# Two of the last chunk's output stores issued by ScalarE in place of SyncE, in a fused S5 state-space and SwiGLU kernel

## The chip, the cores and the metric

The kernel runs on one core of a Trainium2 chip. The metric is the device time of one execution in microseconds; the median of several runs counts. Beside it stands one profiled execution, whose span runs from the program's first to its last instruction.

## What is computed

One sequence of 2048 tokens with 512 features, in bfloat16. The input x is layer-normalized, and the result is the sum of x, a state-space branch and a gated feed-forward branch. Cut to what matters:

```python
xn = layernorm(x)                                  # over the 512 features
# S5 branch: complex diagonal recurrence over time, 512 states
h[t] = Lam_bar * h[t-1] + B_bar @ xn[t]
ssm  = 2 * real(h @ C.T) + xn * Dskip
# feed-forward branch, 1376 hidden features
ffn  = (silu(xn @ w_gate) * (xn @ w_up)) @ w_down
out  = x + ssm + ffn
```

## The kernel before

The tokens are cut into four chunks of 512, and each chunk into four token tiles of 128 (`NT` is 16 tiles, `TPC` is 4 per chunk; tile `n` belongs to chunk `n // 4`). The normalized input is kept transposed in SBUF. For each chunk TensorE multiplies it with the gate and up weights (`gateup_tile`, line 446), and with the input matrix of the recurrence (`bproj_tile`, line 371). ScalarE moves those results out of PSUM and applies silu; VectorE multiplies gate and up, rotates the states, runs the scans over time (line 413) and rotates back. The order of all this is written out by hand: the kernel's last lines queue VectorE's work in pieces, and `pump` takes pieces from that queue beside TensorE's work.

The output of a token tile is a sum in one PSUM tile: the feed-forward products with `w_down` (lines 547, 559 and 587), and then in `out_ssm` (line 606) eight products with the output matrix of the recurrence. For the chunks 0 to 2, ScalarE copies the sum into an SBUF tile `res` (line 618) and GpSimd stores it with an accumulating DMA (line 619), onto x and the skip term that have been put there before.

The last chunk is done otherwise. `out_pair` (line 550) computes the feed-forward part of the chunks 2 and 3 first, then the state-space part of both. In the last chunk x and the skip term lie ready in SBUF (`xn_end`, and for half of the last tile `part_end`), and VectorE adds them as it takes the sum out of PSUM (line 611). The result in `res` is then stored by a plain DMA (line 613). Tiles 0 to 2 of this chunk (n = 12, 13 and 14) are 512 columns wide; the last, n = 15, is computed and stored in three pieces of 256, 128 and 128 columns (`out_blocks`, line 535), so that little is left to do behind its last product. The store of tile 0 is cut in two halves of 256 columns, which have the same piece to wait for.

Which engine issues a store of line 613 is set by its last column: a store that reaches the right edge of the tile (`b == D`) goes out through SyncE, another through ScalarE. Before the change, SyncE so issues the second half of tile 0, tile 1, tile 2 and the last piece of tile 3; ScalarE issues the first half of tile 0 and the first two pieces of tile 3:

```python
for a, b in ((0, D // 2), (D // 2, D)) if i == 0 else ((lo, hi),):
    (nc.sync if b == D else nc.scalar).dma_start(out=out_v[:, n, a:b], in_=res[:, a:b])
```

Each of these two engines has a DMA queue of its own (q1 and q10 in the profile). An engine issues its DMAs in the order of its program, and a DMA waits at its place for what it needs: here for VectorE's addition, and for the DMA that last used its completion semaphore. There are eight such semaphores ("lanes"), which the DMAs of SyncE and ScalarE take in turn, whichever of the two issues; the wait for the lane is an instruction of its own ahead of the DMA. At the program's end SyncE waits for all lanes one after the other, drains, and meets the other engines (these instructions stand under line 877, the launch).

Of the kernel before, what the change touches and what calls it, by code (L numbers as in the profile page):

```python
# [23 lines left out]
def kernel(  # L24
# [17 lines left out]
    nc = tc.nc  # L42
    _, L, D = A_x.shape
# [5 lines left out]
    NT = L // 128  # L49
    NCH = L // CW  # L50
    TPC = CW // 128
# [28 lines left out]
    out_v = out[0].rearrange("(n p) d -> p n d", p=128)  # L80
# [454 lines left out]
    def out_blocks(n):  # L535

        return ((0, D // 2), (D // 2, D - 128), (D - 128, D)) if n == NT - 1 else ((0, D),)
# [12 lines left out]
    def out_pair(c):  # L550

        multiply(0)
        for n in range(c * TPC, (c + 2) * TPC):
            o = bank()
            o_tiles[n] = [o]
            k, i = divmod(n, TPC)
            for lo, hi in col_parts(n):
                for fi in range(FT - 1):
                    nc.tensor.matmul(o[:, lo:hi], lhsT=gu_tiles[k][:, fi, i * 128:(i + 1) * 128],  # L559
                                     rhs=wd_sb[:, fi, lo:hi], start=(fi == 0), stop=False)  # L560
                if lo > 0:
                    out_last(n, o[:, lo:hi], lo, hi, True)
            pump(FT * 0.2163)
        for step in range(3):
            for k in (c, c + 1):
                out_rows(k, step)
        need(f"ssm{c}")
        need("skip")
        for n in range(c * TPC, (c + 1) * TPC):
            out_ssm(n)  # L570
            pump(2 * NQ * 0.2163)
        need(f"ssm{c + 1}")
        n = NT - 1
        o = o_tiles[n][0]
        V.tensor_tensor(out=part_end[:], in0=o[:, D // 2:D], in1=xn_end[:, TPC - 1, D // 2:D], op=ALU.add)
        o_tiles[n] = [o, *(bank((128, hi - lo)) for lo, hi in out_blocks(n)[1:])]
        for n in range((c + 1) * TPC, (c + 2) * TPC):
            out_ssm(n)
# [18 lines left out]
    def out_ssm(n):  # L597
        c, i = divmod(n, TPC)
        if c > 0:
            res = opool.tile([128, D], BF16, name="res")  # L600
        for o, (lo, hi) in zip(o_tiles[n], out_blocks(n)):
            fresh = n == NT - 1 and lo > 0
            o = o[:, 0:hi - lo]
            for part in range(2):
                for q in range(NQ):
                    nc.tensor.matmul(o, lhsT=w_tiles[c][:, part, q, i * 128:(i + 1) * 128],  # L606
                                     rhs=CF[:, part, q, lo:hi], start=(fresh and part == 0 and q == 0),
                                     stop=(c > 0 and part == 1 and q == NQ - 1))
            if c == NCH - 1:
                rest = part_end[:, lo - D // 2:hi - D // 2] if fresh else xn_end[:, i, lo:hi]  # L610
                V.tensor_tensor(out=res[:, lo:hi], in0=o, in1=rest, op=ALU.add)  # L611
                for a, b in ((0, D // 2), (D // 2, D)) if i == 0 else ((lo, hi),):
                    (nc.sync if b == D else nc.scalar).dma_start(out=out_v[:, n, a:b], in_=res[:, a:b])
            elif c > 0:
                out_leave(n, o, res)

    def out_leave(n, o, res):
        nc.scalar.copy(out=res[:], in_=o[:])  # L618
        nc.gpsimd.dma_start(out=out_v[:, n, :], in_=res[:], accum_op=ALU.add)  # L619
# [147 lines left out]
    def out_chunk(c):  # L767

        multiply(0)
        for n in range(c * TPC, (c + 1) * TPC):  # L770
            out_ffn(n)
            pump(FT * 0.2163)
        if c == 0:
            need("ln3")
            up_halves()
            multiply(0)
        need(f"ssm{c}")
        need("cf")
        for n in range(c * TPC, (c + 1) * TPC):
            out_ssm(n)  # L780
            pump(2 * NQ * 0.2163)
# [100 lines left out]
```

## Time and profile before

| | |
|---|---|
| Median of 3 runs | 179.2 us (179.16 to 179.3) |
| The profiled execution's own time | 179.75 us |
| Its span | 178.0 us |
| TensorE clock granted, mean | 0.998 |
| TensorE busy | 172.9 us, 97% |
| VectorE busy | 154.8 us, 87% |
| ScalarE busy | 93.8 us, 53% |
| GpSimd busy | 39.6 us, 22% |
| Line 613, DMA issues | 4 on SyncE, 3 on ScalarE |

The profile knows an engine by a short name: PE is TensorE's matmuls and PEld its weight loads, DVE is VectorE, ACT ScalarE, POOL GpSimd, SP SyncE. A name with a q behind it (ACTq, SPq) is the engine's sequencer: instructions that wait, branch or issue a DMA, which are not counted as busy time. Times inside the profile count from the start of the span. "PE ps L606" is a matmul of line 606 that writes a tile `ps`. The time to landing of a DMA runs from the start of its issue until all of its completion semaphore's increments are in.

### The profile page before, as it was taken

To read this page: it belongs to the slowest core of one execution; us is meant where nothing else is said; L and a number is where in the kernel's file an instruction comes from. 1 tells how busy PE (TensorE), PEld (TensorE's weight loads), DVE (VectorE), ACT (ScalarE), POOL (GpSimd) and SP (SyncE) were. 2 spreads that over 40 slices of the span, in tenths; PEclk is the share of its full clock that TensorE was granted. 3 is DMA by queue.
4 is the path that set the end of the run, shared out by engine and by line. 5 is a ranking of instruction groups with operands and counts; after the bars stand their busy time and mean duration, and the time that the engine had idled before them with its cause. 6 is when DMAs were issued, how large, how long until landed. Compare 5 with 4: busy or idle time off the path is not lost.

```text
span 178.0 us, 2494 instructions
## 1 busy us (share of the span) xinstructions
PE 172.9 (97%) x906; PEld 84.1 (47%) x922; DVE 154.8 (87%) x238; ACT 93.8 (53%) x167; POOL 39.6 (22%) x61
## 2 busy tenths in 40 slices
PE   8999999999999999999999999999999999999992
PEld 2984444444444444444444444444444444474452
DVE  6789997999999995999999999999999999990042
ACT  3468898867399559914966662013766600002300
POOL 6050300000300050000709340014276420002400
PEclk9999999999999999999999999999999999999999
DMA  5998656994041025900450020007479400000752
GB/s 169 305 266 224 131 89 158 349 212 103 17 88 33 0 35 112 353 0 0 54 68 15 9 64 28 0 0 63 55 113 183 79 7 0 0 0 4 80 99 61
DMA packets 30093, 16.13 MB, mean 91 GB/s; under 512 B 19296, under 2 KB 29888, under 8 KB 30048
## 3 DMA queue, kind: packets, MB, share of 16 engines
q1 hardware_dynamic: 25088, 11.80, 28.4%
q0 software_dynamic: 4416, 3.87, 15.6%
q10 hardware_dynamic: 576, 0.30, 0.5%
q8 instruction: 7, 0.11, 0.3%
q14 instruction: 6, 0.05, 0.1%
HBM read 8.42 MB, written 5.24 MB: 77 GB/s over the span
## 4 chain that ended last, share of the span: by engine, by line
PE 97%; issue 1%; DVE 0%
PE ps L446 36%; PE ps L606 15%; PE ps L371 15%; PE ps L559 10%; PE ps L587 10%; PE ps L694 3%; PE ps L671 2%; PE ps L501 2%; PE ps L490 1%; PE ps L594 1%; PE ps L547 1%; PE ps L236 1%; DVE res L611 0%; PE ps L266 0%
## 5 line engine op out<-in xcount | busy, mean ns | idle before, releaser
L446 PE MATMUL ps<-xnT,wg 128*128 128x512 bf16 x144 | 37.8, 379 | 0.4
L446 PE MATMUL ps<-xnT,wu 128*128 128x512 bf16 x145 | 37.3, 379 | 0.0
L413 DVE TENSOR_TENSOR_SCAN g<-r_t,car,u 128x512 bf16<-128x512 f32 x24 | 28.7, 1263 | 0.0
L371 PE MATMUL ps<-xnT,BT 128*128 128x512 bf16 x126 | 28.2, 379 | 0.1
L606 PE MATMUL ps<-CF,wt 128*128 128x512 bf16 (+2 forms) x140 | 27.8, 355 | 0.3 <-issue 0.2
L460 ACT ACTIVATE guT<-ps 128x512 bf16<-128x512 f32 x40 | 24.5, 612 | 6.7 <-PE ps L446 5.2
L461 ACT CAST u<-ps 128x512 bf16<-128x512 f32 x40 | 24.0, 599 | 5.4 <-PE ps L446 5.1
L618 ACT CAST res<-ps 128x512 bf16<-128x512 f32 x12 | 6.7, 594 | 37.5 <-PE ps L606 37.5
L619 POOL DMA_DIRECT2D out_dram<-res x12 | 10.5, 1043 | 59.2 <-ACT res L618 59.2
L446 PEld LDWEIGHTS <-wu 128*128 128x128 bf16 x148 | 14.5, 98 | 17.5
L446 PEld LDWEIGHTS <-wg 128*128 128x128 bf16 x148 | 14.4, 98 | 17.2
L373 ACT CAST u<-ps 128x512 bf16<-128x512 f32 x32 | 18.4, 589 | 5.1 <-PE ps L371 4.9
L606 PEld LDWEIGHTS <-wt 128*128 128x128 bf16 x144 | 13.4, 98 | 14.8 <-issue 0.4
L371 PEld LDWEIGHTS <-BT 128*128 128x128 bf16 x128 | 12.5, 98 | 15.1
L587 PE MATMUL ps<-wd_sb,guT 128*128 128x512 bf16 x78 | 18.0, 379 | 0.1
L559 PE MATMUL ps<-wd_sb,guT 128*128 128x512 bf16 (+1 forms) x89 | 17.5, 355 | 0.1
L211 POOL TENSOR_TENSOR rstd<-ve,neg_half 128x4 f32<-128x4 f32 x3 | 5.2, 1729 | 47.0 <-DVE ve L210 47.0
L186 POOL DMA_DIRECT2D gu_rows<-gu_last x24 | 11.9, 504 | 9.3 <-DVE gu_last L477 6.6
L465 DVE TENSOR_TENSOR guT<-guT,u 128x1024 bf16<-128x1024 bf16 x20 | 13.5, 681 | 0.0
L559 PEld LDWEIGHTS <-guT 128*128 128x128 bf16 x90 | 8.8, 98 | 8.7
L587 PEld LDWEIGHTS <-guT 128*128 128x128 bf16 x80 | 7.8, 98 | 9.4
L611 DVE TENSOR_TENSOR res<-ps,xn_end 128x512 bf16<-128x512 f32 (+1 forms) x4 | 2.5, 625 | 10.6 <-PE ps L606 10.6
(116 smaller groups left out, 199.0 us busy)
## 6 DMA issues: line engine op xcount, KB each, us to landing
out_dram<-in_A_x_dram SPq DMA_DIRECT2D x1, 1536.0 KB, 6.8
out_dram<-res POOLq DMA_DIRECT2D x12, 128.0 KB, 3.1
out_dram<-xall POOLq DMA_DIRECT2D x3, 512.0 KB, 8.2
wd_sb<-in_B_w_down_dram SPq DMA_DIRECT2D x1, 1280.0 KB, 9.8
xall<-in_A_x_dram SPq DMA_DIRECT2D x1, 1024.0 KB, 6.7
wg<-in_B_w_gate_dram SPq DMA_DIRECT2D x1, 512.0 KB, 5.0
wu<-in_B_w_up_dram SPq DMA_DIRECT2D x1, 512.0 KB, 6.0
xall<-in_A_x_dram SPq DMA_DIRECT2D x2, 256.0 KB, 6.1
```

The lines of the kernel that those rows point to most:

```text
L186: nc.gpsimd.dma_start(out=gu_rows[c % 2][i * RT:(i + 1) * RT, p, :], in_=gu_last[c % 3][p * RT:(p + 1) * RT, i * 128:(i + 1) * 128])
L371: nc.tensor.matmul(ps[:], lhsT=BT[:, part, k, q * 128:(q + 1) * 128], rhs=xnT[:, k, c * CW:(c + 1) * CW], start=(k == 0), stop=(k == KD - 1))
L373: nc.scalar.copy(out=u_tiles[c][:, part, q, :], in_=ps[:])
L413: V.tensor_tensor_scan(out=g()[:, part, q, :], data0=r_t[:, q:q + 1].to_broadcast([128, CW]), data1=u_tiles[c][:, part, q, :], initial=ini ...
L446: nc.tensor.matmul(ps[:fs, lo:hi], lhsT=wslice(groups, fi, k), rhs=xnT[:, k, c * CW + lo:c * CW + hi], start=(k == 0), stop=(k == KD - 1))
L460: nc.scalar.activation(out=guT[:fs, fi, :], in_=psg[:fs], func=ACT.Silu)
L461: nc.scalar.copy(out=u_pair[c][:fs, fi % 2, :], in_=psu[:fs])
L465: products.append(lambda: V.tensor_tensor(out=g, in0=g, in1=u, op=ALU.mult))
L559: nc.tensor.matmul(o[:, lo:hi], lhsT=gu_tiles[k][:, fi, i * 128:(i + 1) * 128], rhs=wd_sb[:, fi, lo:hi], start=(fi == 0), stop=False)
L587: nc.tensor.matmul(o[:], lhsT=gu_tiles[c][:, fi, i * 128:(i + 1) * 128], rhs=wd_sb[:, fi, lo:hi], start=(fi == 0), stop=False)
L606: nc.tensor.matmul(o, lhsT=w_tiles[c][:, part, q, i * 128:(i + 1) * 128], rhs=CF[:, part, q, lo:hi], start=(fresh and part == 0 and q == 0 ...
L619: nc.gpsimd.dma_start(out=out_v[:, n, :], in_=res[:], accum_op=ALU.add)
```

## The change

For line 613 the engine is chosen otherwise: SyncE keeps only the second half of tile 0 (n = 12) and the last piece of the last tile (n = 15); tile 1 and tile 2 (n = 13 and 14), each 128 rows of 1024 bytes, are issued by ScalarE.

```diff
@@ -610,7 +610,8 @@
                 rest = part_end[:, lo - D // 2:hi - D // 2] if fresh else xn_end[:, i, lo:hi]
                 V.tensor_tensor(out=res[:, lo:hi], in0=o, in1=rest, op=ALU.add)
                 for a, b in ((0, D // 2), (D // 2, D)) if i == 0 else ((lo, hi),):
-                    (nc.sync if b == D else nc.scalar).dma_start(out=out_v[:, n, a:b], in_=res[:, a:b])
+                    late = b == D and n in (NT - TPC, NT - 1)
+                    (nc.sync if late else nc.scalar).dma_start(out=out_v[:, n, a:b], in_=res[:, a:b])
             elif c > 0:
                 out_leave(n, o, res)
```

In the program as built, the tail of ScalarE's order is then: half of tile 0, tile 1, tile 2, and the first two pieces of tile 3; that of SyncE: the other half of tile 0 and the last piece. The lanes that the stores take are the same as before. Each moved store takes its lane wait along. The other engines' instructions are as before.

## Prediction

> **What bounds the kernel now.** I read the page first, then the chain of work in order of time, then the timeline of the last microseconds engine by engine, then who SyncE waits for there, then the DMA view.
>
> ```profile
> span 178.0 us, 2494 instructions
> ...
> PE 172.9 (97%) x906; PEld 84.1 (47%) x922; DVE 154.8 (87%) x238; ACT 93.8 (53%) x167; POOL 39.6 (22%) x61
> ...
> PE 97%; issue 1%; DVE 0%
> ...
> 171.65 3.02 PE ps L606 x29
> 174.68 0.02 issue
> 174.70 0.29 DVE res L611
> ```
>
> TensorE is busy for 97% of the span, and the chain is TensorE until 174.68 us; then VectorE adds the last 128 columns and is done at 174.70 + 0.29 = 174.99. The span ends at 178.0. The diff touches nothing that TensorE or VectorE waits for (no tile is written again after these stores), so everything up to 174.99 stays, and the question is confined to the 3.0 us behind it. I call the last chunk's token tiles 0 to 3, the halves of tile 0 0a and 0b, and the three pieces of tile 3 3a, 3b and 3c (256, 128 and 128 columns).
>
> The next rows are the timeline: start, duration, engine, line. DVE rows make a piece; an ACTq or SPq row is the engine's sequencer issuing its store.
>
> ```profile
> 169.48 0.69 DVE L611 TENSOR_TENSOR res<-ps,xn_end 128x512 bf16<-128x512 f32 x1 [8.30 <-PE ps L606]
> 170.20 0.38 SPq L613 DMA_DIRECT2D out_dram<-res  x1
> 170.21 0.37 ACTq L613 DMA_DIRECT2D out_dram<-res  x1
> 171.21 0.69 DVE L611 TENSOR_TENSOR res<-ps,xn_end 128x512 bf16<-128x512 f32 x1 [1.03 <-PE ps L606]
> 171.93 0.34 SPq L613 DMA_DIRECT2D out_dram<-res  x1
> 172.99 0.69 DVE L611 TENSOR_TENSOR res<-ps,xn_end 128x512 bf16<-128x512 f32 x1 [1.09 <-PE ps L606]
> 173.71 0.33 SPq L613 DMA_DIRECT2D out_dram<-res  x1
> 173.86 0.42 DVE L611 TENSOR_TENSOR res<-ps,xn_end 128x256 bf16<-128x256 f32 x1 [0.18 <-PE ps L606]
> 174.25 0.29 DVE L611 TENSOR_TENSOR res<-ps,part_end 128x128 bf16<-128x128 f32 x1
> 174.32 0.88 ACTq L613 DMA_DIRECT2D out_dram<-res  x2
> 174.75 0.45 ACTq L613 DMA_DIRECT2D out_dram<-res  x1
> 175.02 0.33 SPq L613 DMA_DIRECT2D out_dram<-res  x1
> ```
>
> Each store is issued 0.03 to 0.04 us after its piece is ready: tile 1 ready at 171.21 + 0.69 = 171.90 and issued at 171.93, tile 2 ready at 173.68 and issued at 173.71, 3a ready at 174.28 and issued at 174.32, 3c ready at 174.99 and issued at 175.02. Only 3b is late: ready at 174.25 + 0.29 = 174.54, issued at 174.75, because ScalarE was still issuing 3a. SyncE is idle from 173.71 + 0.33 = 174.04 until 175.02.
>
> Which store ends last? The DMA view gives the time from issue to landing; the rows are tile 2, 3a, 3b, 3c.
>
> ```profile
> out_dram<-res SPq DMA_DIRECT2D x1, 128.0 KB, 1.7
> ...
> out_dram<-res ACTq DMA_DIRECT2D x1, 64.0 KB, 1.5
> out_dram<-res ACTq DMA_DIRECT2D x1, 32.0 KB, 1.6
> out_dram<-res SPq DMA_DIRECT2D x1, 32.0 KB, 1.5
> ```
>
> Tile 2 lands at 173.71 + 1.7 = 175.4, 3a at 175.8, 3b at 174.75 + 1.6 = 176.35, 3c at 175.02 + 1.5 = 176.52. So **3c ends last, with 3b 0.17 us ahead of it**. Neither store that moves is near the end. Behind 3c comes the closing sequence of SyncE:
>
> ```profile
> SPq L877 <- PEq L877: 0.7, 2, 0.5
> SPq L877 <- DMA out_dram<-res: 0.4, 1, 0.4
> ...
> L877 SPq DRAIN  x3: 7/7/120, 177.0 to 177.5; - x3
> L877 PEldq DRAIN  x2: 13/658/1302, 173.4 to 177.5; - x2
> ...
> L877 ACTq DRAIN  x2: 8/79/150, 175.2 to 177.5; - x2
> ```
>
> SyncE waits for the stores (0.4 us for one of them), and its first drain starts only at 177.0, 0.5 us after 3c has landed. The profile names TensorE's sequencer for that 0.5 us, but TensorE's drain began at 173.4 and took 1.30 us, so it was over at 174.7: the cause of this 0.5 us is unknown. From 177.0 to 178.0 the engines meet and stop, which nothing here changes.
>
> **The change part by part.** It removes two issues and their lane waits from SyncE and adds the same to ScalarE; bytes, shapes and the place of each store in the order stay.
>
> ```profile
> L613 SPq DMA_DIRECT2D out_dram<-res x4: 332/338/383, 170.2 to 175.0; - x4
> L613 ACTq EVENT_SEMAPHORE  x3: 17/17/17, 167.8 to 174.7; - x3
> L613 ACTq DMA_DIRECT2D out_dram<-res x3: 338/371/450, 170.2 to 174.8; - x3
> ```
>
> *SyncE loses* 0.34 + 0.33 = 0.67 us of issuing. Worth nothing on the path: SyncE is idle for 174.04 to 175.02 ahead of 3c and waits for VectorE, and would only be late if this cover of 0.98 us were gone. [...]
>
> *ScalarE gains* two issues and two lane waits of 17 ns (met when they are reached, as the three that ScalarE has already). Tile 1 falls into 171.93 to about 172.3, where ScalarE has been idle since 170.21 + 0.37 = 170.58 and nothing is queued behind it until 173.7: nothing. Tile 2 is the only one with something close behind it. It is issued at 173.71; queued behind it on ScalarE is 3a, and 3b behind that. No row shows a 1024-byte-row store issued by ScalarE. Bounds: 0.33 (the same store on SyncE) to 0.45 (ScalarE's slowest). I take 0.37, ScalarE's median, since that row is the same engine after a pause. From 3a's end at 174.32 + 0.34 = 174.66 to 3b's start there are 0.09 us (the lane wait and its surroundings), so 3a could be issued from 173.71 + 0.37 + 0.09 = 174.17, at the worst from 174.25. It is ready at 174.28 and issued at 174.32 anyway: **not moved, with 0.07 to 0.15 us to spare.** 3b follows 3a as before: not moved.
>
> What can still be lost is a longer issue behind another. 3b, issued directly behind 3a, took 0.45 where 3a took 0.34. If 3a, now 0.2 us behind tile 2, takes 0.45 too, 3b is 0.11 later and lands at 176.46, still before 3c: 0. The far end is SyncE's run of issues at the kernel's start (the last row is the time to landing of line 112's loads):
>
> ```profile
> 0.74 0.40 SPq L121 DMA_DIRECT2D xall<-in_A_x_dram  x1
> ...
> 1.67 0.51 SPq L112 DMA_DIRECT2D wu<-in_B_w_up_dram  x1
> ...
> 4.26 0.51 SPq L112 DMA_DIRECT2D wg<-in_B_w_gate_dram  x1
> ...
> DMA to landing us min/median/max: 3.7/4.3/6.0
> ```
>
> With 0.51 each, tile 2 ends at 174.22 and 3a still starts at about 174.32; 3a takes 0.17 more, 3b 0.06 more, so 3b lands 0.23 later at 176.58, 0.06 behind 3c.
>
> *The transfers.* How much moves on each queue (q1 is SyncE's, q10 ScalarE's: packets, MB, share of 16 engines), in the windows 174.4 to 175.1, 175.1 to 175.6 and, for both queues, 175.6 to 176.2:
>
> ```profile
> q1 hardware_dynamic: 144, 0.13, 53.0%
> ...
> q10 hardware_dynamic: 144, 0.07, 43.6%
> ...
> q10 hardware_dynamic: 144, 0.03, 24.0%
> q1 hardware_dynamic: 144, 0.03, 22.4%
> ```
>
> Tile 2 moves in the first window, 3a in the second, 3b and 3c share the third. Tile 2 has left the engines before 3a begins, so that it is now on 3a's queue costs nothing by this picture. If 3b comes late, it falls upon 3c: 24.0% of 0.6 us is 0.14 us of the engines, the most that it can add to 3c. So the unknowns add from 0 to 0.06 + 0.14 = 0.2 us. Below nothing, 3c could start sooner now that its queue is empty, but tile 2 has moved before 3c is even issued at 175.02, and 3c's 1.5 us is already what 3a takes on ScalarE's empty queue: I allow 0.1 us.
>
> *Sum:* 0 − 0 + 0 = 0 for the profiled execution of 179.75 us (span 178.0 plus 1.75 around it). The runs' median is 179.2, 0.55 below that execution; the same zero is carried over: **179.2 us**, with its own range from 179.0 to 179.45.
>
> **The rivals.**
>
> *Slower: 3b has to wait for tile 2.* With the change ScalarE's queue has three stores under way at 174.75 (tile 2, 3a, 3b), where before it never had more than two within 1.5 us. If a queue keeps 3b back until tile 2 has landed at 175.4, 3b is issued 0.66 us later and lands at 177.01 in place of 176.35, 0.49 behind 3c: 179.7 us. It decides from the point where 3b is over 0.17 us late. For it: 3b's long issue (0.45), as if something were in its way already. Against: SyncE issued its first seven or eight loads between 0.74 and 4.26 us at 0.40 to 0.51 each, with line 112's landings 3.7 to 6.0 us away, so a queue there held several. [...]
>
> *Faster: the 0.5 us before SyncE's drain belongs to its own stores.* If SyncE spends it on clearing up behind the four stores that it issued, with two of them gone half goes, 0.24 us: 178.95 us; if the two big ones were all of it, 0.48 us: 178.7 us. For it: nothing else named is late there. Against: ScalarE's first drain comes right behind 3b's issue (at 175.2, at most 0.15 us long), while 3a and 3b are still moving, so a drain does not wait for stores on that engine.
>
> *The change does not act.* The built program's order shows five stores on ScalarE and two on SyncE, so it does act; that nothing comes of it is the forecast itself.
>
> **How the numbers follow.** About 0.2% (0.36 us) is what a measurement of this kernel can tell from no change. Forecast (0 to +0.2 us, or −0.1): 0.58, all of it within. Slower rival at 179.7: 0.21, all of it slower by over 0.2%. Faster rival: 0.15 for 178.7, faster by over 0.2%, and 0.06 for 178.95, which counts as within. So faster 0.15, same 0.64, slower 0.21. The range from 178.85 to 179.75 takes in the forecast, the slower rival and the half gain, and leaves out the 0.15 at 178.7.
>
> **What would show it.** In the changed profile, line 614 (the diff adds one line above it): five ACTq issues and two SPq; tile 2 issued by ScalarE at about 173.7 and 3a still at about 174.3, 0.04 us after its piece; 3b within 0.1 us of 174.75; 3c last, issued 0.03 us after VectorE's end, landing 1.5 us later; SyncE's first drain 0.5 us behind that. The slower rival would show 3b issued at about 175.4 or landing after 3c. The faster one would show the first drain less than 0.3 us behind 3c's landing. Wrong altogether would be a change ahead of 174.99, where I see no way for the stores to reach.

## The result, and the profile after

The changed kernel takes 178.78 us (median of 14 runs, 178.66 to 179.21), the kernel before 179.31 us beside it (14 runs, 179.16 to 179.79). The ratio is 0.9971 with a 95% interval from 0.9961 to 0.9980: 0.53 us faster, where no change had been forecast and the range ended at 178.85.

Single executions of one kernel differ by up to 0.6 us, and the profiled ones already differ by nearly as much at the end of VectorE's last addition (174.57 to 175.11 us in the ten kernels of this document), so I compare executions from that end on.

The page and the timeline of the changed kernel, with the rows that answer to those of before (ACTq and SPq are the issues of the stores):

```profile
span 177.4 us, 2510 instructions
...
171.25 0.69 DVE L611 TENSOR_TENSOR res<-ps,xn_end 128x512 bf16<-128x512 f32 x1 [1.03 <-PE ps L606]
171.97 0.34 ACTq L614 DMA_DIRECT2D out_dram<-res  x1
173.03 0.69 DVE L611 TENSOR_TENSOR res<-ps,xn_end 128x512 bf16<-128x512 f32 x1 [1.09 <-PE ps L606]
173.75 0.34 ACTq L614 DMA_DIRECT2D out_dram<-res  x1
174.36 0.34 ACTq L614 DMA_DIRECT2D out_dram<-res  x1
174.74 0.29 DVE L611 TENSOR_TENSOR res<-ps,part_end 128x128 bf16<-128x128 f32 x1 [0.16 <-PE ps L606]
174.79 0.39 ACTq L614 DMA_DIRECT2D out_dram<-res  x1
175.06 0.34 SPq L614 DMA_DIRECT2D out_dram<-res  x1
```

The stores do what the prediction said. ScalarE issues tile 1 and tile 2 in 0.34 us each and 3a at 174.36, not late. VectorE ends at 175.03, 3c is issued 0.03 us later and lands last. From VectorE's end to 3c's landing nothing is gained: 1.52 us before, 1.49 us after.

What is gained lies behind that. These are the instructions of SyncE's closing sequence in windows cut around 3c's landing (their durations in ns, then the start of the first and the last): first the kernel before, the last two lane waits and then the first drain,

```profile
L877 SPq EVENT_SEMAPHORE  x2: 28/28/28, 176.4 to 176.5; - x2
...
L877 SPq DRAIN  x1: 120/120/120, 177.0 to 177.0; - x1
```

and the same of the changed kernel:

```profile
L878 SPq EVENT_SEMAPHORE  x2: 28/28/28, 176.3 to 176.5; - x2
...
L878 SPq DRAIN  x1: 13/13/13, 176.6 to 176.6; - x1
...
SPq L878 <- PEq L878: 0.7, 2, 0.5
```

Both kernels see 3c's landing at 176.5. Before, the first drain begins 0.47 us behind the end of that wait and takes 120 ns; after, it begins 0.04 us behind and takes 13 ns. That is 0.47 − 0.04 + 0.12 − 0.01 = 0.54 us, the whole of the difference between the medians. The last row is a trap. The same row, 0.7, 2 and 0.5, stands in the view of before, and there too it is not the gap ahead of the first drain: it holds SyncE's two waits for releases, and the 0.5 us are the one in the last instruction of the program. The row names TensorE, but what stands just ahead of SyncE's last instruction in both kernels is GpSimd's release (177.88 and 177.92 us before, 177.34 and 177.41 after). For the first drain of before the profile shows no wait at all.

### The profile page after: what moved, and what is told of

Its sections match the earlier page's. It is cut to its first block, busy times and chain, and to the rows that moved or that the text cites. A ratio compares the mean times of both kernels' runs of the same rounds, so it can differ in the third digit from the quotient of the medians.

```text
span 177.4 us, 2510 instructions
## 1 busy us (share of the span) xinstructions
PE 173.1 (98%) x922; PEld 83.1 (47%) x922; DVE 154.6 (87%) x238; ACT 93.8 (53%) x167; POOL 39.6 (22%) x61
## 4 chain that ended last, share of the span: by engine, by line
PE 94%; DMA 3%; SPq 2%; issue 0%; DVE 0%
PE ps L446 36%; PE ps L606 16%; PE ps L371 16%; PE ps L559 10%; PE ps L587 10%; DMA wu<-in_B_w_up_dram 3%; PE ps L501 2%; PE ps L695 2%; PE ps L490 1%; PE ps L594 1%; PE ps L547 1%; SPq L112 1%; SPq L126 0%; SPq L127 0%; SPq L121 0%
## 5 line engine op out<-in xcount | busy, mean ns | idle before, releaser
L446 PE MATMUL ps<-xnT,wu 128*128 128x512 bf16 x148 | 38.0, 379 | 0.0
```

What stands on the lines that cost most here:

```text
L446: nc.tensor.matmul(ps[:fs, lo:hi], lhsT=wslice(groups, fi, k), rhs=xnT[:, k, c * CW + lo:c * CW + hi], start=(k == 0), stop=(k == KD - 1))
```

## What could explain it

The prediction had named this 0.5 us as unknown and had given it, in its faster rival, to the stores that SyncE issues (*stores theory*: SyncE clears up behind them, and with two of four gone the stall goes). The two traces show something else. Counted from the start of the span, SyncE has 84 instructions before and 80 after (two stores and their two lane waits are gone). The stalled instruction is the 80th: before, the first closing drain. After, the 80th is the very last one, the wait for the final release. It comes 0.48 us behind the end of the one ahead of it, hardly later than in the kernel before (0.46 us, with no stall there), for it waits that long for GpSimd's release anyway; but SyncE takes up this release 0.025 us behind ScalarE, where before it was 0.005 us ahead of it. The other thing that goes with it is a packet on the DMA queue that the page lists as "q14 instruction". In the page of before this queue and its neighbour are

```profile
q8 instruction: 7, 0.11, 0.3%
q14 instruction: 6, 0.05, 0.1%
```

(packets, MB: 0.05 MB in 6 packets are some 8 KB each). One q14 packet starts 0.62 us after the start of the stalled drain before, at 177.65, and one 0.63 us after the start of SyncE's last instruction in the changed kernel, at 178.04. These are their rows, before in the window from 177.6 to 178.05 and after in the one from 178 to 178.6:

```profile
q14 instruction: 1, 0.01, 5.3%
...
q14 instruction: 1, 0.01, 5.7%
```

So the rival is the *place theory*: at a fixed place of its program, counted in its own instructions, SyncE stands still for about half a microsecond (0.47 us ahead of the first drain before), whatever instruction is there. The change took four instructions out ahead of that place, so that another instruction met it. Which engine issues the stores would then be worth nothing. That the packet brings SyncE instructions, and that the stall goes with fetching them, is my reading of the queue's name and of the 0.62 and 0.63 us; no trace shows what is in the packet.

## The experiments

The first two undo the count without touching the stores, and undo the stores without the count. A drain on SyncE with nothing to wait for stands in for an instruction; it is put behind the copy of x that SyncE issues at about 70 us, after which SyncE has nothing to do for 99 us.

**Changed kernel, four drains more on SyncE.**

```diff
     nc.sync.dma_start(out=out[0, 0:(NT - TPC) * 128, :], in_=A_x[0, 0:(NT - TPC) * 128, :])
+    for _ in range(4):
+        nc.sync.drain()
```

> The changed kernel with four empty drains added to SyncE's program at about 71 us, where SyncE has nothing to do for 99 us. Place theory: SyncE stalls for about 0.5 us at a fixed place of its instruction stream, its 80th instruction in the profile, whatever stands there (the first closing drain in the kernel before, the very last instruction in the changed one, where it is hidden). Four more instructions push the first closing drain back onto that place: the gap ahead of it is 0.47 us again, and the time is that of the kernel before, 179.3 us, ratio 1.000. Stores theory: the 0.5 us belonged to the stores that SyncE issues; it still issues only two, so the gap stays 0.04 us and the time 178.8 us, ratio 0.997.

Measured: 179.29 us, ratio 1.0003 [0.9993, 1.0012] to the kernel before. The gain is gone with both stores still on ScalarE. In its trace the lane waits and the first drain stand as in the kernel before:

```profile
L880 SPq EVENT_SEMAPHORE  x2: 28/28/28, 176.2 to 176.4; - x2
...
L880 SPq DRAIN  x1: 106/106/106, 176.9 to 176.9; - x1
```

The stores theory fails here.

**Kernel before, four drains more on SyncE** (the same two lines, stores as before).

> The kernel before, stores where they were, with the same four empty drains on SyncE at about 71 us. Place theory: the 80th instruction is now the wait for 3a's lane, whose stall of 0.47 us (from 175.75 to about 176.2) is over before 3b lands at 176.35, so it is hidden: first closing drain 0.04 us behind the last lane wait, 178.8 us, ratio 0.997 with no store moved. Stores theory: nothing changes, gap 0.47 us, 179.3 us, ratio 1.000.

Measured: 179.00 us, ratio 0.9976 [0.9965, 0.9987]; the fastest of its runs took 178.70 us (the changed kernel's 178.66, that of the kernel before 179.16). Most of the gain comes with no store moved. The stall is in the trace, but early: in the window from 175.85 to 176.35 there is one lane wait, which starts 0.47 us behind the end of the one at 175.81, and the rest of the row runs through.

```profile
L879 SPq EVENT_SEMAPHORE  x1: 28/28/28, 175.8 to 175.8; - x1
...
L879 SPq EVENT_SEMAPHORE  x1: 28/28/28, 176.3 to 176.3; - x1
...
L879 SPq EVENT_SEMAPHORE  x1: 28/28/28, 176.6 to 176.6; - x1
L879 SPq DRAIN  x1: 7/7/7, 176.7 to 176.7; - x1
```

That wait asks for tile 2's lane, not 3a's as my expectation had it (I had counted one too far); it ends before 3c lands at 176.62, so it costs nothing.

**Only tile 1 on ScalarE.**

```diff
-                    (nc.sync if b == D else nc.scalar).dma_start(out=out_v[:, n, a:b], in_=res[:, a:b])
+                    late = b == D and n != NT - 3
+                    (nc.sync if late else nc.scalar).dma_start(out=out_v[:, n, a:b], in_=res[:, a:b])
```

> Only tile 1's store goes to ScalarE, tile 2's stays with SyncE: two instructions fewer on SyncE than before. Place theory: the 80th instruction is the first release wait of the closing meeting, so the first drain comes 0.04 us behind the last lane wait, but SyncE takes up the release some 0.33 us later than the other engines do; about 179.1 us, ratio 0.999. Stores theory: half of the stall is gone, the gap ahead of the first drain is about 0.25 us; 179.0 to 179.1 us, and the other engines and SyncE take up the release together.

Measured: 178.99 us, ratio 0.9975 [0.9964, 0.9985], fastest 178.71: more than the 0.999 that the place theory gave. The stall is where it was expected, on the first release wait, two instructions behind the first drain:

```profile
L878 SPq DRAIN  x2: 7/10/13, 176.4 to 176.5; - x2
L878 SPq EVENT_SEMAPHORE  x1: 28/28/28, 176.3 to 176.3; - x1
...
L878 POOLq DRAIN  x2: 46/74/102, 176.7 to 177.0; - x2
L878 ACTq EVENT_SEMAPHORE  x1: 17/17/17, 176.6 to 176.6; - x1
...
L878 POOLq EVENT_SEMAPHORE_RANGE_CLEAR  x1: 139/139/139, 176.8 to 176.8; - x1
L878 SPq EVENT_SEMAPHORE  x1: 17/17/17, 177.0 to 177.0; - x1
```

SyncE takes up the release at 176.95, ScalarE at 176.6. What I had left out: between the first release and the last meeting GpSimd clears semaphores (its drains and the clear, 176.7 to 177.0), and SyncE's 0.33 us pass beside that. From 3c's landing to the end of the span it is 0.97 us here, 0.93 in the changed kernel and 1.47 before. The size of the expectation was wrong, the place was right; and the gap ahead of the first drain is 0.05 us, not the 0.25 of the stores theory.

**Two other stores on ScalarE: tile 0's second half and tile 1.**

```diff
-                    (nc.sync if b == D else nc.scalar).dma_start(out=out_v[:, n, a:b], in_=res[:, a:b])
+                    late = b == D and n >= NT - 2
+                    (nc.sync if late else nc.scalar).dma_start(out=out_v[:, n, a:b], in_=res[:, a:b])
```

> Two other stores go to ScalarE: tile 0's second half and tile 1; tile 2 (the late, large one) stays with SyncE ahead of 3c. SyncE has four instructions fewer, as in the changed kernel. Place theory: which stores leave does not matter, gap 0.04 us, 178.8 us, ratio 0.997. Stores theory, with the late large store as the one that has to be cleared up: gap still 0.25 to 0.47 us, 179.0 to 179.3 us, ratio 0.9985 to 1.000.

Measured: 178.74 us, ratio 0.9967 [0.9955, 0.9978]. The first drain follows the last lane wait at once, as in the changed kernel:

```profile
L878 SPq EVENT_SEMAPHORE  x1: 28/28/28, 176.1 to 176.1; - x1
L878 SPq DRAIN  x1: 7/7/7, 176.1 to 176.1; - x1
```

Which two stores leave SyncE does not matter; that it has four instructions fewer does (178.74 us here, 178.78 with the change).

**Kernel before, twenty drains on SyncE.** The same two lines with `range(20)`.

> The kernel before with twenty empty drains on SyncE at about 71 us. Place theory: the 80th instruction is now one of these drains, so the stall falls into SyncE's 99 us of idle time and the block of instructions is fetched at about 73 us in place of 177.6; the closing sequence runs through, first drain 0.04 us behind the last lane wait, ratio 0.997, as with the change, with all four stores on SyncE. Stores theory: as the kernel before, gap 0.47 us, ratio 1.000.

Measured: 178.84 us, ratio 0.9968 [0.9957, 0.9980], with all four stores on SyncE: the gain of the change without the change. This run also shows the stall by itself, among equal instructions that wait for nothing. These are the drains in the windows from 72.1 to 72.25 and from 72.25 to 72.8:

```profile
L841 SPq DRAIN  x3: 7/7/7, 72.1 to 72.2; - x3
...
L841 SPq DRAIN  x1: 121/121/121, 72.7 to 72.7; - x1
```

The first drain, right behind the issue of the copy, takes 0.37 us; the others follow each other after some 0.05 us and take 7 ns, except the 18th, which is SyncE's 80th instruction: it comes 0.46 us behind the end of the 17th and takes 121 ns. And the closing sequence, the last lane waits and the first drain, runs through:

```profile
L879 SPq EVENT_SEMAPHORE  x2: 28/28/28, 176.3 to 176.5; - x2
L879 SPq DRAIN  x1: 7/7/7, 176.5 to 176.5; - x1
```

The instruction packet at the end of the span is gone too; one goes out in the window from 75.4 to 76.4 instead (3.2 us behind the stalled drain and not 0.6):

```profile
q14 instruction: 1, 0.01, 1.9%
```

SyncE's 1.5 MB copy, which lands at 77.35, is then under way. From 73.9 to 76.5 us its queue takes 77.1% of the 16 DMA engines:

```profile
q1 hardware_dynamic: 27, 0.79, 77.1%
```

That the copy holds the packet back is a guess of mine; no run shows it.

**Changed kernel, twenty drains on SyncE.**

> The changed kernel with the same twenty drains. Place theory: the stall falls into the idle time as well; the last instruction of SyncE, which in the changed kernel comes about 0.03 us behind the other engines' because the stall sits on it, comes with them; 178.75 us, ratio 0.997, the same as the changed kernel within what can be measured. If the move of the stores is worth something of its own, this kernel is faster than the one before with twenty drains.

Measured: 178.81 us, ratio 0.9974 [0.9965, 0.9984]. The 18th drain is the late one again (72.30 us, 0.46 us behind the end of the 17th, 119 ns), and the closing sequence runs through (the row of its first two drains, then that of the last lane wait ahead of them):

```profile
L880 SPq DRAIN  x2: 7/7/7, 176.2 to 176.2; - x2
L880 SPq EVENT_SEMAPHORE  x1: 28/28/28, 176.1 to 176.1; - x1
```

With the stall out of the way in both, four stores on SyncE (178.84) and two (178.81) take the same time: the move of the stores is worth nothing of its own that can be measured. Nor does taking the stall off the last instruction give more than the changed kernel has.

**Kernel before, one drain on SyncE.** `range(1)`.

> The kernel before with a single empty drain on SyncE. Place theory: the 80th instruction is the wait for 3c's lane, which now starts 0.47 us behind the wait for 3b's (3b lands 0.17 us ahead of 3c), so about 0.3 us of the stall stay visible where 0.5 were: about 179.1 us, ratio 0.9985 to 0.999, and the first drain follows within 0.05 us. Stores theory: 179.3 us, ratio 1.000, gap 0.47 us.

Measured: 179.14 us, ratio 0.9987 [0.9979, 0.9996]. The wait for 3c's lane starts 0.47 us behind the end of that for 3b's; the first drain follows at once:

```profile
L879 SPq EVENT_SEMAPHORE  x1: 28/28/28, 175.9 to 175.9; - x1
...
L879 SPq EVENT_SEMAPHORE  x1: 28/28/28, 176.4 to 176.4; - x1
...
L879 SPq DRAIN  x1: 26/26/26, 176.5 to 176.5; - x1
```

3c landed at 176.07 in this execution, so some 0.35 us of the stall are visible and the rest lies under 3c's flight; from the landing to the end it is 1.28 us, between the 1.47 of before and the 0.91 without a stall. A stall that costs less because part of it is covered is what the place theory says and the stores theory can't.

**The control: four drains on ScalarE.**

```diff
+    for _ in range(4):
+        nc.scalar.drain()
```

> The control: the kernel before with four empty drains on ScalarE, not on SyncE, at the same place of the program. Place theory: SyncE's stream is not touched, its 80th instruction is the first closing drain, gap 0.47 us, ratio 1.000 (or a little over, if the drains hold ScalarE up). If instead any small disturbance of the program made the kernel faster, this one would be faster too.

Measured: 179.31 us, ratio 1.0003 [0.9995, 1.0012]. SyncE's first drain is as late as before:

```profile
L879 SPq DRAIN  x1: 115/115/115, 177.0 to 177.0; - x1
```

The control also tells something about the packets. One q14 packet that starts between 165.3 and 166.3 us in the nine other kernels starts at 143.10 us here, in the window from 142.6 to 143.6,

```profile
q14 instruction: 1, 0.01, 2.0%
```

and none starts from 165 to 167. In the kernel before and in this one ScalarE has started 191 instructions when that packet starts (193 in the changed kernel, at 166.28 us); four of them are drains here, so it reaches that count earlier. SyncE's packet stays at 177.65. So in this run the one packet went with the place in ScalarE's own stream, and the other with the place in SyncE's. Whether ScalarE stands still there too can't be seen, for it waits for TensorE at that point in both kernels.

All together, by where SyncE's 80th instruction falls (us from 3c's landing to the end, in the profiled execution):

| kernel | the 80th instruction | landing to end | ratio |
|---|---|---|---|
| before | first closing drain | 1.47 | 1 |
| four drains on ScalarE | first closing drain | 1.46 | 1.0003 |
| changed, +4 on SyncE | first closing drain | 1.46 | 1.0003 |
| before, +1 | wait for 3c's lane | 1.28 | 0.9987 |
| tile 1 only | first release wait | 0.97 | 0.9975 |
| changed | last instruction | 0.93 | 0.9971 |
| before, +4 | wait for tile 2's lane | 0.92 | 0.9976 |
| two other stores | last instruction | 0.92 | 0.9967 |
| before, +20 | a drain at 72.7 us | 0.91 | 0.9968 |
| changed, +20 | a drain at 72 us | 0.91 | 0.9974 |

What is shown: in eight of the ten kernels SyncE's 80th instruction starts 0.46 to 0.49 us behind the end of the 79th, whatever that instruction is and later than what it waits for explains, and this costs what of it nothing else covers. In the other two (changed, two other stores) the 80th is the last one, which waits for GpSimd nearly as long anyway; there the stall can be seen only in that SyncE takes up the release 0.03 to 0.04 us behind ScalarE, while in the eight it is 0.004 to 0.005 us ahead. A q14 packet moves with it: it starts 0.61 to 0.68 us behind the start of SyncE's 80th instruction, 3.2 and 3.3 us in the two kernels with twenty drains. That the stall has to do with fetching instructions is argued from this packet and its queue's name alone; what SyncE does in that half microsecond stays open. No version tried here is measurably faster than the changed kernel: the ones without a visible stall lie between 178.74 and 179.00 us, and the intervals of their ratios overlap.

## Why the prediction was wrong

- *Everything up to VectorE's end stays:* right. No engine ahead of it moved by the change.
- *SyncE's 0.67 us of issuing are worth nothing:* right as a term, SyncE still waits for VectorE ahead of 3c. The two experiments with twenty drains put it at 178.84 against 178.81 us.
- *ScalarE takes both issues without delaying 3a or 3b:* right. An issue took 0.34 us where I took 0.37; 3a is issued 0.03 us after its piece.
- *Tile 2 ahead of 3a on one queue costs nothing:* right, 3a still lands 1.6 us after its issue and 3b 1.5; so the slower rival did not occur.
- *3c ends last and lands 1.5 us after its issue:* right.
- *The sum, 0 − 0 + 0:* wrong. The step that failed is the removal itself: I counted what the removed instructions cost and gave that as nothing, but not that the four instructions taken out of SyncE's program moved all that follow, so that its 80th, where it stalls, was no longer the first drain but its last instruction. The 0.47 us gap stood in the prediction as of unknown cause, and I left it in the sum as a constant with a chance of 0.21 that it would shrink. It measured 0.04 us in the changed kernel, and with the shorter drain 0.54 us fell away behind 3c's landing.
- *The gap's row:* misread. I took the row "SPq L877 <- PEq L877: 0.7, 2, 0.5" for the gap ahead of the first drain and rejected TensorE as its cause. The 0.5 in it is SyncE's wait in the program's last instruction; for the drain the profile shows no wait, so SyncE itself was the place to look.
- *The faster rival:* its whole-gap form at 178.7 us gave the size that came, with 0.15. Its mechanism, SyncE clearing up behind its own stores, was wrong: the kernel before with twenty drains keeps all four stores and has no gap. Its sign "first drain less than 0.3 us behind 3c's landing" came true for another reason (0.08 us).

The trace of before alone could have told more: the q14 packet 0.62 us behind the unexplained gap was there, in a window in which nothing else moves, and so was the fact that SyncE's lane waits, where they have nothing to wait for, follow one another after 0.03 to 0.05 us.

## What to carry to other kernels

Where a gap in a sequencer's row has no releaser that fits, look for an instruction packet of the DMA queues behind it (0.61 to 0.68 us in eight kernels here, 3.2 and 3.3 us in two), and count which instruction of that engine it is. If the gap is on the path, a few instructions more or fewer on that engine may move it to where the engine waits anyway, as four fewer did here (179.31 to 178.78 us); a gain or a loss of about that size from an edit that takes instructions away may have nothing to do with what they did. Test it by adding as many empty instructions in an idle stretch.

## What had not been expected of the hardware

SyncE stood still for 0.46 to 0.49 us at its 80th instruction in the eight kernels where that can be seen, even when it was a drain with nothing to wait for, 100 us ahead of the end; and a drain that met the stall took 106 to 121 ns, where the first closing drain took 7 to 26 without it. And at the end of this program GpSimd's clearing of semaphores covers a late SyncE: taking up the first release 0.33 us late cost 0.04 us at the end of the span.
